# A third joint product in seven weight pairs, with six loads' weight sums kept in DRAM

## Chip, cores, metric

One core of a Trainium2 chip. The metric is the device time of one execution in microseconds (us), lower is better. Kernels are compared only within the same rounds.

## The reference

A linear-attention block gated by a SwiGLU feed-forward block, on 2048 tokens of 1024 features:

```python
xn = _layernorm(x)
s  = _A_ref(xn, A_wqkv, A_wo)          # q, k, v; phi = elu+1; o = q(kv)/q(z); @ wo
g  = silu((silu(xn @ w_gate) * (xn @ w_up)) @ w_down)   # w_gate, w_up: 1024 x 3584
out = x + s * g
```

## The kernel before

The kernel works on two token halves, one after the other. Each weight product is a two-level scheme of the Strassen kind: a "set" has seven products (1 to 7) in place of eight, each of 4 matmuls of 512 columns. Two sets that share their input form a "pair" (gate n, up n, q n, or s n, the attention output). Products 1 and 5 of the two sets are done together, as an inner scheme of the same kind: seven inner products of two matmuls of 256 columns, 14 short matmuls in place of 8 long ones, 3584 columns in place of 4096.

```python
class Joint:                                   # one joint product, four steps a..d
    def step(self, part):
        if part == 0:
            self.grp(1, y, 0, True); self.grp(5, y, 1)
            act(... ps[x][:, 0:256], ps[y][:, 0:256], Identity)   # ACT copies
            act(... self.s, ps[y][:, 256:512], Identity)
        elif part == 1: self.grp(6, y, 0); self.grp(2, x, 0); tt(... ALU.add)
        elif part == 2: self.grp(7, y, 0); self.grp(3, x, 1); tt(... ALU.add); self.put(0, x)
        elif part == 3: self.grp(4, y, 0); self.put(1, y)
# the order in which a pair's head is threaded into the tail of the pair ahead
LINK = "7_0 nj1a 3_0 7_1 nj1b nj5a 3_1 nj1c nj5b 4_0 nj1d nj5c 4_1 n2_0 nj5d n6_0 n2_1 n6_1".split()
```

The price is sums of weights on VectorE. For each 1 MB load, `wload` makes four sums of 128x1024, and for each joint product four inner sums of 128x256:

```python
sums({(k, i): v[...] ...}, [cv[:, q] for q in range(4)], [sr], cr)
for m in joint:                                # joint = (1, 5)
    sums(A, [tv[:, q] for q in range(4)], [r], tr)
```

A planner written in Python orders all instructions at build time, with WINDOW (how many TensorE groups it looks ahead) and LEAD (how early transfers are issued) as constants.

Of the kernel before, what the change touches and what calls it, by code (L numbers as in the profile page):

```python
# [9 lines left out]
ACT = mybir.ActivationFunctionType  # L10
# [4 lines left out]
KB = 1024  # L15
# [19 lines left out]
class Plan:  # L35
# [91 lines left out]
    def tune(self):  # L127

        self.place()
        front = 0.0  # L130
        while True:
            prev, last, work, at = {}, {}, 0.0, None
# [187 lines left out]
def build_kernel(nc, A_x, A_wqkv, A_wo, B_w_gate, B_w_up, B_w_down, out, WINDOW=6, NWARM=15, NPE=2, LEAD=12.0):  # L320
# [12 lines left out]
    with ExitStack() as es:  # L333
# [250 lines left out]
        class Set:  # L584
# [4 lines left out]
            def __init__(self, ops, evac, dring):  # L589
                self.ops, self.evac, self.dring, self.direct = ops, evac, dring, None  # L590

# [16 lines left out]

            def put1(self, a):
                self.a = a  # L610
                self.b = balloc()
                act([bank_r[a]], [bank_r[self.b]], ps[self.b][:, :], ps[a][:, :], ACT.Identity)

            def put5(self, e):
# [93 lines left out]
        TAIL = "7_0 3_0 7_1 4_0 3_1 4_1".split()  # L708
        LINK = "7_0 nj1a 3_0 7_1 nj1b nj5a 3_1 nj1c nj5b 4_0 nj1d nj5c 4_1 n2_0 nj5d n6_0 n2_1 n6_1".split()
        last_pair = [None]  # L710

        def feed(pair):

            prev = last_pair[0]
            if pair is None or not pair.joint:
                if prev is not None:
                    for w in TAIL:
                        prev.do(w)
                if pair is not None:
                    for w in HEAD:  # L720
                        pair.do(w)
            else:
                for w in LINK:
                    if w[0] == "n":
                        pair.do(w[1:])
                    elif prev is not None:
                        prev.do(w)
            last_pair[0] = pair

# [385 lines left out]

        def wload(src, joint, dt=BF16, rd=(), inh=(0, 0)):
            if inh[0]:
# [10 lines left out]
            if inh[1]:  # L1128
                cs, keys = strips("T1", FP16)
                cv = cs.rearrange("p (m w) (kt n) -> p m w kt n", w=2, n=128)  # L1130
                cr = [Region(keys[2 * q] + keys[2 * q + 1]) for q in range(4)]
            else:
                c = cmb_ring.take()
                cv = c.ap(FP16).rearrange("p (m w kt n) -> p m w kt n", m=4, w=2, n=128)
                cr = [c.sub(q * 2 * KB, 2 * KB).r for q in range(4)]
            sums({(k, i): v[:, :, 4 * k:4 * k + 4, i * 128:i * 128 + 128] for k in range(2) for i in range(2)},
                 [cv[:, q] for q in range(4)], [sr], cr)

            def block(m):
# [8 lines left out]
            inner = {}  # L1148
            for m in joint:
                bl, r = block(m)  # L1150
                t = in_ring.take()
                tv = t.ap(FP16).rearrange("p (m kt n) -> p m kt n", m=4, n=128)
                tr = [t.sub(q * KB // 2, KB // 2).r for q in range(4)]
                A = {(k, i): bl[:, i, 2 * k:2 * k + 2, :] for k in range(2) for i in range(2)}
                sums(A, [tv[:, q] for q in range(4)], [r], tr)
                inner[m] = (A, r, tv, tr)
# [18 lines left out]

        def x_inner(v, xin=xin, places=IN_AT):

            for m, at in zip((1, 5), places):
                ap, r = v[XOF[m]]
                B = {(k, j): ap[:, 2 * k:2 * k + 2, 256 * j:256 * j + 256] for k in range(2) for j in range(2)}  # L1180
                t = [(a.at(o, KB, FP16).rearrange("p (k t) -> p k t", t=256), a.reg(o, KB)) for a, o in at]
                tt([r], [t[1][1]], t[1][0], B[1, 1], B[0, 1], ALU.subtract, True)
                tt([r], [r], B[0, 1], B[0, 1], B[0, 0], ALU.subtract, True)
                tt([r], [t[0][1]], t[0][0], B[1, 1], B[0, 1], ALU.subtract, True)
                tt([r, t[0][1]], [t[2][1]], t[2][0], B[1, 0], t[0][0], ALU.subtract, True)
                xin[m] = {1: (B[0, 0], r), 2: (B[1, 0], r), 3: (B[1, 1], r), 5: (B[0, 1], r), 6: t[0], 7: t[1], 4: t[2]}

        def joint_of(jstat, s0, s1, xin=xin):
            def ops(m):
                def f(k):  # L1190
                    ws, wr = jstat(m, k)
                    xa, xr = xin[m][k]
                    return [(ws[q], xa[:, q, :]) for q in range(2)], [wr, xr]
                return f
            return {"1": Joint(ops(1), lambda w, b: (s0, s1)[w].put1(b)),
                    "5": Joint(ops(5), lambda w, b: (s0, s1)[w].put5(b))}
# [17 lines left out]
        def q_load(p, s):  # L1214
            return wload(wqkv_v[:, :, s * 512:(s + 1) * 512], QJ[p][s])

# [4 lines left out]
        def q_pair(p, s, stats, at, go=True):  # L1221
# [8 lines left out]
            s0, s1 = (xset(stat, w, XV[p], evac(w), d_ring) for w in range(2))  # L1230
            pair = Pair(s0, s1, joint_of(jstat, s0, s1) if QJ[p][s] else None, at)
            if go:
# [55 lines left out]

        def gu_load(k, n):
            return wload((wg_v if k == "g" else wu_v)[:, :, n * 512:(n + 1) * 512], (1, 5), inh=(1, 1) if gate[0] and (k, n) == ("g", 0) else (0, 0))  # L1290

        sgs = {}

        def gu_pair(p, kind, n, stats, at):
# [9 lines left out]
            def ev_u(w):  # L1304
                def f(i, j, ap, r, bank):
                    s = sgs[w, i, j]
                    o, orr = hb(2 * n + w, "R%d%d" % (i, j))
                    act([r], [orr], o, ap, ACT.Identity)
                    tt([orr, s.r], [orr], o, o, s.ap(FP16), ALU.mult, True)
                    if w == 1 and (i, j) == (0, 0) and n in TJ_CUT:  # L1310
                        tj_first(p, TJ_CUT[n], n + 1)
                    if w == 1 and (i, j) == (0, 1):
                        h_sums(2 * n)
                return f

            def direct(w):
                def f(i, j, b, s5):
                    s = sgs[w, i, j]
                    o, orr = hb(2 * n + w, "R%d%d" % (i, j))
                    tt([bank_r[b], s5.r], [orr], o, ps[b][:, :], s5.ap(F32), ALU.add)  # L1320
                    tt([orr, s.r], [orr], o, o, s.ap(FP16), ALU.mult, True)
                return f
            s0, s1 = (xset(stat, w, XV[p], (ev_g if kind == "g" else ev_u)(w), d_ring) for w in range(2))
            if kind == "u":
                s0.direct, s1.direct = direct(0), direct(1)
            feed(Pair(s0, s1, joint_of(jstat, s0, s1), at))

# [6 lines left out]

        def s_load(n):
            return wload(m_v[:, :, n * 512:(n + 1) * 512], (1, 5), FP16, [named("mscr", n, g, k) for g in (0, 4) for k in range(4)])

# [15 lines left out]
        GB = 3584  # L1353
        TJ_CUT = {2: 0, 5: 3, 6: 6}
        NU = NPAIR // 2
# [305 lines left out]
        def down(p):  # L1661
# [7 lines left out]
            for seq, prev, nxt in ((IN_D, last_pair[0], d0), (ON_D, d0, d1), (END_D if p else OUT_D, d1, None)):  # L1669
                if seq == END_D:  # L1670
                    PL.cushion = 4.0
                for t in seq.split():
# [16 lines left out]
                    elif t[0] == "n":  # L1689
                        nxt.do(t[1:])  # L1690
                    else:
                        prev.do(t)
            last_pair[0] = nxt

# [8 lines left out]
        def pump(n):  # L1703
            while lq and len(got) < n and lq[0][1] <= gate[0]:
                k, p, s = lq.popleft()
                got[k, p, s] = q_load(p, s) if k == "q" else s_load(s) if k == "s" else gu_load(k, s)

# [10 lines left out]
        def turn_pass():  # L1718
# [9 lines left out]
            gate[0] = 1  # L1728
            raw_ring.__init__([(X, 0), (W, 0 * KB), (X, 0), (W, 8 * KB), (W, 16 * KB)] + [(W, 0), (W, 8 * KB), (W, 16 * KB)] * 5, 8 * KB)
            cmb_ring.__init__([(X, 8 * KB), (X, 8 * KB)] + [(W, 24 * KB), (W, 32 * KB)] * 8, 8 * KB)  # L1730
            in_ring.__init__([(W, 14 * KB), (TM, 8 * KB), (W, 24 * KB), (W, 26 * KB), (W, 42 * KB), (W, 44 * KB)]
# [6 lines left out]
        for p in range(2):  # L1738
            for k, n in order:
# [4 lines left out]
                if p == 0 and (k, n) in (("g", 0), ("u", 0), ("q", 1)):  # L1744
                    at = {"6_1": [build_m]}
                    if k == "u":
                        at["6_0"] = [build_m]
                if (p, k, n) == (0, "g", 1):
                    for q in range(4):
                        dma([P.reg(q * 4 * KB, 4 * KB)], [named("xscr", q)], x_scr[q], P.at(q * 4 * KB, 4 * KB, FP16),  # L1750
                            dsem("xp%d" % q), 512 * KB, after=PL.lastpe)
                if (k, n) == ("u", 1):
                    at = {"j1d": [partial(recip, p)]}
                if (k, n) == ("g", 2):
                    at = {"j1a": [partial(normalise_part, p, 0, 0)], "2_1": [partial(normalise_part, p, 0, 1)]}
                if (k, n) == ("u", 2):
                    at = {"j1a": [partial(normalise_part, p, 1, 0)], "2_1": [partial(normalise_part, p, 1, 1)], "4_1": [partial(combos, QV)]}
                if (k, n) == ("g", 3):
                    at = {"2_1": [partial(x_inner, QV, qin, QIN_AT)]}
                if last_pair[0] is not None and (p, k, n) == (1, "q", 0):  # L1760
                    pass
                elif k == "q":
                    q_pair(p, n, st, at)
                elif k == "s":
# [75 lines left out]
```

## Time and profile before

| | before |
|---|---|
| median, first runs | 712.4 us (711.8 to 713.31) |
| span of the profiled execution | 710.2 us |
| PE (TensorE) busy | 704.5 us, 4181 matmuls |
| VectorE (DVE) busy | 631.2 us, 1534 instructions |
| ScalarE (ACT) busy | 424.9 us |
| moved by DMA | 98.64 MB |

### The profile page before, as it was taken

Reading aid. Unit: us, or ns where it says so; the run is one execution under the profiler, and the core shown is the slowest. Engines: PE = TensorE matmul, PEld = TensorE weight load, DVE = VectorE, ACT = ScalarE, POOL = GpSimd, SP = SyncE. Lnnn points to the kernel's source line nnn. Section 1 sums busy time; section 2 is a strip of 40 time slices with the busy share of each in tenths; the row PEclk is TensorE's granted clock in tenths of the full one; section 3 lists DMA queues with packets and bytes.
Section 4 is the critical chain, followed back from the end, with each engine's and each line's share of the span. In section 5 each row is a group of like instructions: output and inputs, shape, how many; then the busy total and the mean of one; then the engine's idle time right before and its main releaser. Section 6 shows DMA issues by size and latency. Waiting matters only on the chain.

```text
span 710.2 us, 11444 instructions
## 1 busy us (share of the span) xinstructions
PE 704.5 (99%) x4181; PEld 388.1 (55%) x4181; DVE 631.2 (89%) x1534; ACT 424.9 (60%) x827; POOL 13.0 (2%) x34
## 2 busy tenths in 40 slices
PE   8999999999999999999999999999999999999997
PEld 3444445555555555556556455555555555565654
DVE  6999858989999999998958999999999999798863
ACT  5788766988679676664212257876886756531212
POOL 2111000000000000000000000000000000000000
PEclk9999999999999999999999999999999999999999
DMA  9654133346664253326498854322716241646763
GB/s 301 143 95 115 31 118 120 119 133 194 175 181 147 96 160 108 110 63 174 123 243 212 219 133 148 111 68 94 208 60 193 75 149 60 181 138 160 144 156 96
DMA packets 140871, 98.64 MB, mean 139 GB/s; under 512 B 34960, under 2 KB 137872, under 8 KB 140816
## 3 DMA queue, kind: packets, MB, share of 16 engines
q1 hardware_dynamic: 139472, 96.69, 49.1%
q10 hardware_dynamic: 1344, 1.25, 0.5%
q8 instruction: 32, 0.52, 0.3%
q14 instruction: 23, 0.19, 0.1%
HBM read 77.59 MB, written 12.71 MB: 127 GB/s over the span
## 4 chain that ended last, share of the span: by engine, by line
PE 98%; DMA 1%; SPq 0%; issue 0%; DVE 0%; ACT 0%
PE ps L309 98%; DMA H<-in_A_wqkv_dram 1%; PE ps L316 0%; DVE TM L453 0%; SPq L456 0%; SPq L760 0%; ACT TM L442 0%
## 5 line engine op out<-in xcount | busy, mean ns | idle before, releaser
L309 PE MATMUL ps<-X,W 128*128 128x512 f16 (+2 forms) x1348 | 282.6, 349 | 0.0
L442 ACT ACTIVATE TM<-ps 128x512 f16<-128x512 f32 (+3 forms) x386 | 202.7, 554 | 100.8 <-PE ps L309 97.3
L309 PE MATMUL ps<-H,W 128*128 128x512 f16 (+2 forms) x1096 | 218.6, 351 | 0.1
L309 PEld LDWEIGHTS ps<-X,W 128*128 128x128 f16 (+1 forms) x1348 | 130.0, 98 | 101.6 <-ACT H L442 1.0
L453 DVE TENSOR_TENSOR W<-W 128x256 f16<-128x256 f16 (+5 forms) x400 | 178.8, 479 | 2.7 <-PE ps L309 1.9
L309 PEld LDWEIGHTS ps<-H,W 128*128 128x128 f16 (+1 forms) x1096 | 105.9, 98 | 95.4 <-DVE ps L453 1.1
L453 DVE TENSOR_TENSOR ps<-ps,TM 128x256 f32<-128x256 f32 (+1 forms) x250 | 131.4, 527 | 14.8 <-PE ps L309 11.5
L442 ACT ACTIVATE ps<-ps 128x512 f32<-128x512 f32 (+1 forms) x174 | 85.7, 493 | 89.9 <-PE ps L309 89.4
L442 ACT ACTIVATE H<-ps 128x512 f16<-128x512 f32 (+1 forms) x132 | 78.5, 605 | 37.8 <-PE ps L309 37.8
L309 PE MATMUL ps<-P,W 128*128 128x256 f16 (+1 forms) x492 | 94.5, 318 | 0.0
L453 DVE TENSOR_TENSOR H<-H 128x1024 f16<-128x1024 f16 (+5 forms) x130 | 73.7, 581 | 0.7 <-ACT H L442 0.5
L442 ACT ACTIVATE TM<-TM 128x512 f16<-128x512 f32 (+1 forms) x70 | 44.0, 631 | 45.6 <-DVE TM L453 45.1
L309 PEld LDWEIGHTS ps<-P,W 128*128 128x128 f16 (+1 forms) x492 | 47.9, 98 | 27.0 <-ACT TM L442 0.8
L309 PE MATMUL ps<-W 128*128 128x256 f16 (+1 forms) x326 | 61.2, 282 | 0.0
L453 DVE TENSOR_TENSOR H<-H,TM 128x512 f16<-128x512 f16 (+1 forms) x120 | 48.0, 417 | 8.5 <-ACT H L442 8.3
L453 DVE TENSOR_TENSOR TM<-ps,TM 128x512 f32<-128x512 f32 (+3 forms) x63 | 41.6, 660 | 12.9 <-PE ps L309 12.0
L309 PEld LDWEIGHTS ps<-W 128*128 128x128 f16 (+1 forms) x326 | 31.1, 98 | 31.0 <-DVE ps L453 0.8
L309 PE MATMUL ps<-H,X 128*128 128x512 bf16 (+1 forms) x150 | 35.2, 379 | 0.4 <-DMA H<-in_A_wqkv_dram 0.4
L453 DVE TENSOR_TENSOR TM<-TM 128x512 bf16<-128x512 f16 (+2 forms) x73 | 29.2, 412 | 6.1 <-ACT TM L442 4.4
L309 PE MATMUL ps<-H,P 128*128 128x512 bf16 (+1 forms) x110 | 26.8, 379 | 0.0
L453 DVE TENSOR_TENSOR H<-ps,TM 128x512 f16<-128x512 f32 (+1 forms) x35 | 24.0, 686 | 2.2 <-PE ps L309 1.3
L453 DVE TENSOR_TENSOR TM<-TM,W 128x512 f16<-128x512 f16 (+1 forms) x39 | 14.1, 363 | 11.8 <-ACT TM L442 11.7
(111 smaller groups left out, 417.0 us busy)
## 6 DMA issues: line engine op xcount, KB each, us to landing
W<-in_B_w_up_dram SPq DMA_DIRECT2D x14, 1024.0 KB, 5.6
W<-in_B_w_gate_dram SPq DMA_DIRECT2D x13, 1024.0 KB, 5.3
W<-in_B_w_down_dram SPq DMA_DIRECT2D x14, 896.0 KB, 6.1
H<-r_scratch SPq DMA_DIRECT2D x32, 128.0 KB, 3.9
W<-m_scratch SPq DMA_DIRECT2D x4, 1024.0 KB, 5.4
s_scratch<-TM SPq DMA_DIRECT2D x32, 128.0 KB, 2.0
TM<-in_A_x_dram SPq DMA_DIRECT2D x16, 256.0 KB, 4.0
W<-in_A_x_dram SPq DMA_DIRECT2D x15, 256.0 KB, 3.4
```

The lines of the kernel that those rows point to most:

```text
L309: last = h.matmul(o, l, r, start=st, stop=sp, skip_group_check=True)
L442: q = PL.op("act", reads, writes, lambda h: h.activation(o, i, func, **kw), nel(o) / (1000.0 if "bias" in kw or not isinstance(kw.get("sca ...
L453: return dve(reads, writes, lambda h: h.tensor_tensor(o, a, b, op), nel(o), 1.92 if fast else 0.96)
```

## The change

In the second token half, seven pairs do product 2 jointly too. To make room on VectorE for the extra inner sums and additions, six loads store their weight sums to DRAM in the first half and load them in the second. The core of the diff:

```diff
+LINK3 = "7_0 nj1a 3_0 7_1 nj1b nj5a 3_1 nj1c nj5b 4_0 nj1d nj5c 4_1 nj2a nj5d n6_0 nj2b n6_1 nj2c".split()
+w_scr = nc.dram_tensor("w_scratch", [18, 128, 4 * KB], FP16)
+i_scr = nc.dram_tensor("i_scratch", [18, 2, 128, KB], FP16)
+TWO = [('g', 1), ('u', 1), ('g', 3), ('g', 4), ('u', 4), ('g', 5), ('u', 5)]
+NOSP = [('q', 0), ('g', 0), ('u', 0), ('q', 1), ('g', 2), ('u', 2), ('s', 1), ('u', 6), ('g', 6), ('u', 5), ('g', 5), ('u', 4)]
+CH, IH, put = {}, {}, {}
 ...
+            keep = (kind, n) not in NOSP
+            if p and keep:
+                dma([named("ws", kept)], [cl], call, ...)          # second half: load the sums
+            else:
+              sums(...)
+              if keep:                                              # first half: store them,
+                put.setdefault((kind, n), []).append((CH.get((kind, n), "j1a"), lambda: dma(   # at step j1a
+                    [cl], [named("ws", kept)], w_scr[kept], call, ...)))
-            for m in joint:
+            for m in joint + ((2,) if p and (kind, n) in TWO else ()):
 ...  (the inner blocks of products 1 and 5 likewise; one spare copy of product 1 goes to SBUF
 ...   in place of PSUM and is added to product 2 by VectorE; buffers of the second half move;
 ...   the planner's improvement loop is capped at 90 rounds)
```

NOSP lists the loads that are not kept; what remains is gate 1, 3, 4, up 1, 3 and s 0.

More of the change, by code (lines that the diff above doesn't have):

```diff
@@ L130, in tune @@
         front = 0.0
-        while True:
+        for _ in range(90):
             prev, last, work, at = {}, {}, 0.0, None
@@ L589, in __init__ @@
             def __init__(self, ops, evac, dring):
-                self.ops, self.evac, self.dring, self.direct = ops, evac, dring, None
+                self.ops, self.evac, self.dring, self.direct, self.two = ops, evac, dring, None, False
             def out(self, i, j, b):
@@ L609, in put1 @@
             def put1(self, a):
+                if self.two:
+                    self.b = a
+                    self.s1 = s1_ring.take()
+                    act([bank_r[a]], [self.s1.r], self.s1.ap(F32), ps[a][:, :], ACT.Identity)
+                    return
                 self.a = a
@@ L612, in put1, with put2 @@
                 act([bank_r[a]], [bank_r[self.b]], ps[self.b][:, :], ps[a][:, :], ACT.Identity)
+            def put2(self, x):
+                if self.direct is not None:
+                    self.direct(0, 0, x, self.s1)
+                    bfree(x)
+                    return
+                d = d2_ring.take()
+                tt([bank_r[x], self.s1.r], [d.r], d.ap(F32), ps[x][:, :], self.s1.ap(F32), ALU.add)
+                bfree(x)
+                self.evac(0, 0, d.ap(F32), d.r, None)
             def put5(self, e):
@@ L722, in feed @@
             else:
-                for w in LINK:
+                for w in LINK3 if "2" in pair.joint else LINK:
                     if w[0] == "n":
@@ L727, in feed @@
                         prev.do(w)
+                    if w == "7_0" and prev is not None and prev.joint and "2" in prev.joint:
+                        prev.do("j2d")
             last_pair[0] = pair
@@ L1114, in strips, with wload @@
                     [hb(n, nm)[1].keys for n in range(8)])
-        def wload(src, joint, dt=BF16, rd=(), inh=(0, 0)):
+        w_scr = nc.dram_tensor("w_scratch", [18, 128, 4 * KB], FP16)
+        i_scr = nc.dram_tensor("i_scratch", [18, 2, 128, KB], FP16)
+        s1_ring, in2_ring, d2_ring = (Places([(a, o * KB) for a, o in at], 2 * KB) for at in (
+            [(H, 36), (H, 38), (H, 36), (H, 38), (H, 36), (H, 38), (H, 72), (H, 74), (H, 72), (H, 74), (H, 72), (H, 74), (H, 72), (H, 74)],
+            [(H, 42), (H, 44), (H, 42), (H, 68), (H, 70), (H, 76), (H, 78)],
+            [(H, 46), (X, 14), (H, 46), (X, 14), (H, 80), (H, 82), (H, 80), (H, 82)]))
+        TWO = [('g', 1), ('u', 1), ('g', 3), ('g', 4), ('u', 4), ('g', 5), ('u', 5)]
+        NOSP = [('q', 0), ('g', 0), ('u', 0), ('q', 1), ('g', 2), ('u', 2), ('s', 1), ('u', 6), ('g', 6), ('u', 5), ('g', 5), ('u', 4)]
+        CH, IH, put = {}, {}, {}
+        def wload(src, joint, tag, dt=BF16, rd=(), inh=(0, 0)):
+            p, kind, n = tag
+            kept = {"g": 0, "u": 7, "s": 14, "q": 16}[kind] + n
             if inh[0]:
@@ L1128, in wload @@
             if inh[1]:
-                cs, keys = strips("T1", FP16)
+                cs, keys = strips((None, "T1", "T3")[inh[1]], FP16)
                 cv = cs.rearrange("p (m w) (kt n) -> p m w kt n", w=2, n=128)
                 cr = [Region(keys[2 * q] + keys[2 * q + 1]) for q in range(4)]
+                call, csem = cs, dsem("wch%d" % inh[1])
             else:
@@ L1135, in wload @@
                 cr = [c.sub(q * 2 * KB, 2 * KB).r for q in range(4)]
-            sums({(k, i): v[:, :, 4 * k:4 * k + 4, i * 128:i * 128 + 128] for k in range(2) for i in range(2)},
+                call, csem = c.ap(FP16), dsem("wc%s%d" % (c.a.name, c.off // KB))
+            cl = Region(sum((r.keys for r in cr), ()))
+            keep = (kind, n) not in NOSP
+            if p and keep:
+                kv = w_scr[kept]
+                dma([named("ws", kept)], [cl], call, kv.rearrange("p (b t) -> p b t", t=512) if inh[1] else kv, csem, 1024 * KB)
+            else:
+              sums({(k, i): v[:, :, 4 * k:4 * k + 4, i * 128:i * 128 + 128] for k in range(2) for i in range(2)},
                  [cv[:, q] for q in range(4)], [sr], cr)
+              if keep:
+                put.setdefault((kind, n), []).append((CH.get((kind, n), "j1a"), lambda: dma(
+                    [cl], [named("ws", kept)], w_scr[kept], call, dsem("wk%s%d" % (c.a.name, c.off // KB)), 1024 * KB,
+                    after=PL.lastpe)))
             def block(m):
@@ L1148, in wload @@
             inner = {}
-            for m in joint:
+            for m in joint + ((2,) if p and (kind, n) in TWO else ()):
                 bl, r = block(m)
-                t = in_ring.take()
+                t = (in2_ring if m == 2 else in_ring).take()
                 tv = t.ap(FP16).rearrange("p (m kt n) -> p m kt n", m=4, n=128)
@@ L1154, in wload @@
                 A = {(k, i): bl[:, i, 2 * k:2 * k + 2, :] for k in range(2) for i in range(2)}
-                sums(A, [tv[:, q] for q in range(4)], [r], tr)
+                place = "%s%d" % (t.a.name, t.off // KB)
+                held = named("wi", kept, m)
+                if p and m != 2 and keep:
+                    dma([held], [t.r], t.ap(FP16), i_scr[kept, m // 5], dsem("wi" + place), 256 * KB)
+                else:
+                    sums(A, [tv[:, q] for q in range(4)], [r], tr)
+                    if not p and keep:
+                        put.setdefault((kind, n), []).append((IH.get((kind, n), "j%da") % m, partial(
+                            dma, [t.r], [held], i_scr[kept, m // 5], t.ap(FP16), dsem("wj" + place), 256 * KB)))
                 inner[m] = (A, r, tv, tr)
@@ L1174, in build_kernel, with x_inner @@
         xin, qin = {}, {}
-        def x_inner(v, xin=xin, places=IN_AT):
-            for m, at in zip((1, 5), places):
+        def x_inner(v, xin=xin, places=IN_AT, ms=(1, 5)):
+            for m, at in zip(ms, places):
                 ap, r = v[XOF[m]]
@@ L1182, in x_inner, with joint_of @@
                 tt([r], [t[1][1]], t[1][0], B[1, 1], B[0, 1], ALU.subtract, True)
-                tt([r], [r], B[0, 1], B[0, 1], B[0, 0], ALU.subtract, True)
-                tt([r], [t[0][1]], t[0][0], B[1, 1], B[0, 1], ALU.subtract, True)
+                f, fr = t[3] if len(t) > 3 else (B[0, 1], r)
+                tt([r], [fr], f, B[0, 1], B[0, 0], ALU.subtract, True)
+                tt([r, fr], [t[0][1]], t[0][0], B[1, 1], f, ALU.subtract, True)
                 tt([r, t[0][1]], [t[2][1]], t[2][0], B[1, 0], t[0][0], ALU.subtract, True)
-                xin[m] = {1: (B[0, 0], r), 2: (B[1, 0], r), 3: (B[1, 1], r), 5: (B[0, 1], r), 6: t[0], 7: t[1], 4: t[2]}
-        def joint_of(jstat, s0, s1, xin=xin):
+                xin[m] = {1: (B[0, 0], r), 2: (B[1, 0], r), 3: (B[1, 1], r), 5: (f, fr), 6: t[0], 7: t[1], 4: t[2]}
+        def joint_of(jstat, s0, s1, xin=xin, two=False):
             def ops(m):
@@ L1194, in ops @@
                 return f
-            return {"1": Joint(ops(1), lambda w, b: (s0, s1)[w].put1(b)),
+            s0.two = s1.two = two
+            js = {"2": Joint(ops(2), lambda w, b: (s0, s1)[w].put2(b))} if two else {}
+            return {**js, "1": Joint(ops(1), lambda w, b: (s0, s1)[w].put1(b)),
                     "5": Joint(ops(5), lambda w, b: (s0, s1)[w].put5(b))}
@@ L1214, in q_load @@
         def q_load(p, s):
-            return wload(wqkv_v[:, :, s * 512:(s + 1) * 512], QJ[p][s])
+            return wload(wqkv_v[:, :, s * 512:(s + 1) * 512], QJ[p][s], (p, "q", s))
         def pq_tile(g, j):
@@ L1230, in q_pair @@
             s0, s1 = (xset(stat, w, XV[p], evac(w), d_ring) for w in range(2))
-            pair = Pair(s0, s1, joint_of(jstat, s0, s1) if QJ[p][s] else None, at)
+            pair = Pair(s0, s1, joint_of(jstat, s0, s1, two=p == 1 and ("q", s) in TWO) if QJ[p][s] else None, at)
             if go:
@@ L1287, in hb2, with gu_load @@
             return v, Region(hb(n, nm)[1].keys + hb(n + 1, nm)[1].keys)
-        def gu_load(k, n):
-            return wload((wg_v if k == "g" else wu_v)[:, :, n * 512:(n + 1) * 512], (1, 5), inh=(1, 1) if gate[0] and (k, n) == ("g", 0) else (0, 0))
+        def gu_load(p, k, n):
+            return wload((wg_v if k == "g" else wu_v)[:, :, n * 512:(n + 1) * 512], (1, 5), (p, k, n), inh={("g", 0): (1, 1), ("u", 0): (0, 2)}.get((k, n), (0, 0)) if p else (0, 0))
         sgs = {}
@@ L1309, in f @@
                     tt([orr, s.r], [orr], o, o, s.ap(FP16), ALU.mult, True)
-                    if w == 1 and (i, j) == (0, 0) and n in TJ_CUT:
-                        tj_first(p, TJ_CUT[n], n + 1)
+                    if w == 1 and (i, j) == (0, 0) and n in TJ_CUT[p]:
+                        tj_first(p, TJ_CUT[p][n], n + 1)
                     if w == 1 and (i, j) == (0, 1):
@@ L1321, in f @@
                     tt([orr, s.r], [orr], o, o, s.ap(FP16), ALU.mult, True)
+                    if w == 1 and (i, j) == (0, 0) and n in TJ_CUT[p]:
+                        tj_first(p, TJ_CUT[p][n], n + 1)
                 return f
@@ L1325, in gu_pair @@
                 s0.direct, s1.direct = direct(0), direct(1)
-            feed(Pair(s0, s1, joint_of(jstat, s0, s1), at))
+            feed(Pair(s0, s1, joint_of(jstat, s0, s1, two=p == 1 and (kind, n) in TWO), at))
         def h_sums(n):
@@ L1332, in h_sums, with s_load @@
             tt([v["R11"][1], v["T1"][1]], [v["T2"][1]], v["T2"][0], v["R11"][0], v["T1"][0], ALU.subtract, True)
-        def s_load(n):
-            return wload(m_v[:, :, n * 512:(n + 1) * 512], (1, 5), FP16, [named("mscr", n, g, k) for g in (0, 4) for k in range(4)])
+        def s_load(p, n):
+            return wload(m_v[:, :, n * 512:(n + 1) * 512], (1, 5), (p, "s", n), FP16, [named("mscr", n, g, k) for g in (0, 4) for k in range(4)])
         st_ring = Places([(TM, o * KB) for o in (20, 24, 21, 25)], KB)
@@ L1353, in build_kernel @@
         GB = 3584
-        TJ_CUT = {2: 0, 5: 3, 6: 6}
+        TJ_CUT = ({2: 0, 5: 3, 6: 6},) * 2
         NU = NPAIR // 2
@@ L1692, in down @@
                         prev.do(t)
+                        if t == "7_0" and isinstance(prev, Pair) and "2" in prev.joint:
+                            prev.do("j2d")
             last_pair[0] = nxt
@@ L1705, in pump @@
                 k, p, s = lq.popleft()
-                got[k, p, s] = q_load(p, s) if k == "q" else s_load(s) if k == "s" else gu_load(k, s)
+                got[k, p, s] = q_load(p, s) if k == "q" else s_load(p, s) if k == "s" else gu_load(p, k, s)
         pump(2)
@@ L1728, in turn_pass @@
             gate[0] = 1
-            raw_ring.__init__([(X, 0), (W, 0 * KB), (X, 0), (W, 8 * KB), (W, 16 * KB)] + [(W, 0), (W, 8 * KB), (W, 16 * KB)] * 5, 8 * KB)
-            cmb_ring.__init__([(X, 8 * KB), (X, 8 * KB)] + [(W, 24 * KB), (W, 32 * KB)] * 8, 8 * KB)
+            raw_ring.__init__([(X, 0), (W, 0 * KB), (X, 8 * KB), (W, 8 * KB), (W, 16 * KB)] + [(W, 0), (W, 8 * KB), (W, 16 * KB)] * 5, 8 * KB)
+            cmb_ring.__init__([(X, 8 * KB)] + [(W, 24 * KB), (W, 32 * KB)] * 8, 8 * KB)
             in_ring.__init__([(W, 14 * KB), (TM, 8 * KB), (W, 24 * KB), (W, 26 * KB), (W, 42 * KB), (W, 44 * KB)]
@@ L1744, in build_kernel @@
                 if p == 0 and (k, n) in (("g", 0), ("u", 0), ("q", 1)):
-                    at = {"6_1": [build_m]}
+                    at["6_1"] = [build_m]
                     if k == "u":
                         at["6_0"] = [build_m]
+                for w, fn in put.pop((k, n), ()):
+                    at.setdefault(w, []).append(fn)
                 if (p, k, n) == (0, "g", 1):
@@ L1752, in build_kernel @@
                 if (k, n) == ("u", 1):
-                    at = {"j1d": [partial(recip, p)]}
+                    at.update({"j1d": [partial(recip, p)]})
                 if (k, n) == ("g", 2):
-                    at = {"j1a": [partial(normalise_part, p, 0, 0)], "2_1": [partial(normalise_part, p, 0, 1)]}
+                    for w, fn in (("j1a", partial(normalise_part, p, 0, 0)), ("2_1", partial(normalise_part, p, 0, 1))):
+                        at.setdefault(w, []).insert(0, fn)
                 if (k, n) == ("u", 2):
-                    at = {"j1a": [partial(normalise_part, p, 1, 0)], "2_1": [partial(normalise_part, p, 1, 1)], "4_1": [partial(combos, QV)]}
+                    for w, fn in (("j1a", partial(normalise_part, p, 1, 0)), ("2_1", partial(normalise_part, p, 1, 1)), ("4_1", partial(combos, QV))):
+                        at.setdefault(w, []).insert(0, fn)
                 if (k, n) == ("g", 3):
-                    at = {"2_1": [partial(x_inner, QV, qin, QIN_AT)]}
+                    at.setdefault("2_1", []).append(partial(x_inner, QV, qin, QIN_AT))
+                if p == 1 and (k, n) in TWO and "2_1" in at:
+                    at["6_1"] = at.pop("2_1")
                 if last_pair[0] is not None and (p, k, n) == (1, "q", 0):
@@ L1762, in build_kernel @@
                 elif k == "q":
+                    if (p, n) == (1, 1) and TWO:
+                        x_inner(XV[1], places=(((X, 1536), (X, 2560), (X, 5 * KB), (X, 6 * KB)),), ms=(2,))
                     q_pair(p, n, st, at)
```

## The prediction

> **What bounds the kernel now.** I read the page from the top: busy times, slices, then the chain that ended last, and after that the list of who waited for whom on PE.
>
> ```profile
> PE 704.5 (99%) x4181; PEld 388.1 (55%) x4181; DVE 631.2 (89%) x1534; ACT 424.9 (60%) x827; POOL 13.0 (2%) x34
> PE   8999999999999999999999999999999999999997
> PE 98%; DMA 1%; SPq 0%; issue 0%; DVE 0%; ACT 0%
> ```
>
> ```profile
> PE ps L309 <- DVE TM L574: 1.0, 1, 1.0
> PE ps L316 <- DVE W L798: 0.7, 1, 0.7
> PE ps L316 <- DVE TM L453: 0.6, 1, 0.6
> PE ps L309 <- DMA H<-in_A_wqkv_dram: 0.4, 1, 0.4
> ```
>
> The four lines are all the waits that PE has in the whole execution: 2.7 us, from the warm-up and the first tiles. After that PE never waits; 98% of the chain is matmuls. DVE at 89% is near full but hides behind PE. A busy PE need not be at its best pace, so I look at the pace: the PE timeline, columns start, length, instructions.
>
> ```profile
> 445.20 0.38 PE L309 MATMUL ps<-P,X 128*128 128x256 f16 x2
> 445.42 0.38 PE L309 MATMUL ps<-P,W 128*128 128x256 f16 x2
> 445.63 0.38 PE L309 MATMUL ps<-P,TM 128*128 128x256 f16 x2
> 445.85 1.03 PE L309 MATMUL ps<-P,X 128*128 128x512 f16 x4
> 446.72 0.38 PE L309 MATMUL ps<-W 128*128 128x256 f16 x2
> ```
>
> Lengths overlap, so the starts count. Six 256-column matmuls start between 445.20 and 445.85: 0.65/6 = 0.108 us each. Four of 512 columns take 446.72 - 445.85 = 0.87 us: 0.217 each. The pace is proportional to the columns; no semaphore wait shows between the groups. The loads in the DMA queue's timeline give the length of one gate/up pair, because each is issued when the pair three places earlier leaves its buffer:
>
> ```profile
> 579.90 0.38 SPq L456 DMA_DIRECT2D W<-in_B_w_gate_dram  x1
> 591.61 0.38 SPq L456 DMA_DIRECT2D W<-in_B_w_up_dram  x1
> ```
>
> 11.71 us. From the code, one pair is two Strassen sets of seven products; products 1 and 5 of the two sets are done jointly, as an inner seven-product scheme of 14 matmuls of 256 columns each, and the other five are 2 x 4 matmuls of 512 columns. That is 40 x 0.2165 + 28 x 0.1085 = 8.66 + 3.04 = 11.70 us: the pair is nothing but its matmuls' columns.
>
> **What the Trainium skill says.** "TensorE: Matmul & The Clock Gate", section "Back-to-back issue gap", gives N/2.4 + 2.5 ns for a warm matmul by itself: 215.8 ns at 512 and 109.2 at 256. The trace agrees within 1% (217, 108). The same section says a sustained stream reaches about 131 ns at 512; this trace does not (217). "Perfetto Trace Analysis", section "Identifying the Most-Contended Engine", warns that matmul busy share does not measure the distance to the roofline; hence the column count above. "VectorE: DVE Perf Modes", section "The perf-mode tier table", has tensor_tensor at twice the base rate for 16-bit SBUF operands and at the base rate if any is in PSUM: here 128x512 takes 417 ns all in SBUF and 686 to 696 with a PSUM operand. "DMA: Bandwidth & Descriptors", section "Bandwidth", has 6.15 us for 1 MB from HBM; here the 1 MB weight loads land 5.3 to 5.6 us after issue.
>
> **The change, part by part.** I counted the instructions of the two built programs.
>
> (a) Joint product two. Seven pairs of the second token half (gate 1, 3, 4, 5 and up 1, 4, 5) replace 8 matmuls of 512 columns by 14 of 256. The counts fit: 512-column matmuls 2469 to 2413 (-56), 256-column ones 1386 to 1484 (+98). In PE time: -56 x 0.2165 + 98 x 0.1085 = -12.12 + 10.63 = -1.49 us with the trace's pitches; with the skill's two numbers -12.08 + 10.70 = -1.38. I take -1.45. All of it lies on the path, since the chain is PE. (The change was announced to me as eight pairs; the counts show seven in this build.)
>
> (b) Kept sums. Six loads (gate 1, 3, 4, up 1, 3, and one half of the second-token attention output) store their four 128x1024 sums and two inner blocks to DRAM in the first half and load them in the second. DVE loses 24 instructions of 128x1024 and 48 of 128x256. Back to back these cost 0.60 and 0.20 us (two of 0.68 us end after 1.28): 24 x 0.60 + 48 x 0.20 = 24.0 us. DMA gains 6 x (1 MB + 2 x 256 KB) each way, 36 issues, 9.4 MB written and 9.4 read.
>
> (c) What the joint product costs beside PE. DVE: 28 inner sums of 128x256 (5.6), 14 additions of 128x256 from PSUM (14 x 0.34 = 4.8), 14 final additions of 128x512 from PSUM (14 x 0.61 = 8.5), four sums of x (1.4): 20.3 us. DVE is thus about 3.7 us lighter in total, 12 instructions fewer. ACT: 14 more copies of 128x256 (381 ns), 6 fewer evacuations of 128x512 (0.60): +1.7 us on an engine that is 60% busy. Both are beside PE and worth nothing by themselves; the purpose of (b) is to make room for (c).
>
> (d) The planner's improvement loop is now capped at 90 rounds; I counted 23 rounds in the build of the kernel before and 22 in the changed one. The cap does nothing.
>
> Sum: -1.45 us on 712.4 gives 710.95 us if no new wait appears.
>
> **The rivals.** The windows of the second half show what stands near its limit (stretch, length, then busy PE, PEld, DVE, ACT, POOL, clock, DMA share, GB/s):
>
> ```profile
> 503.50:515.00 11.50, 11.50 (x69) 6.58 (x68) 11.49 (x31) 9.95 (x20) 0.00 (x0) 1.00 0.86 210
> 549.50:561.00 11.50, 11.50 (x69) 6.49 (x67) 11.50 (x30) 7.58 (x16) 0.00 (x0) 1.00 0.45 143
> 584.00:595.50 11.50, 11.50 (x68) 6.48 (x67) 10.39 (x27) 7.75 (x16) 0.00 (x0) 1.00 0.27 84
> 607.00:618.50 11.50, 11.50 (x69) 6.48 (x68) 7.78 (x15) 7.75 (x16) 0.00 (x0) 1.00 0.54 152
> ```
>
> *DVE becomes the bound locally.* Up 4, gate 5 and up 5 have joint product two but still form all their sums: each adds about 4 x 0.20 + 2 x 0.34 + 2 x 0.61 = 2.7 us to an 11.5 us pair, 8.1 us for the three. Gate 4 adds 2.7 and saves 4 x 0.60 + 8 x 0.20 = 4.0. From 545 to 618 us that is +6.8 us net against some 6.6 us that DVE had idle there: full to the brim. For it: DVE at 11.50 of 11.50. Against it: windows of 100% DVE already run today with no PE wait, and weight sums can be made ahead of time. If PE followed DVE I would expect 0.5 to 2 us back: 711.5 to 713.
>
> *DMA is late.* The three loads in a row gate 3, up 3 and the attention half fall at 498 to 533 us, where the reciprocals' broadcasts already make 0.86. At about 300 GB/s each kept load (1.57 MB) adds some 5.2 us of DMA time; the three windows from 492 had 19 us of 34.5 in use (0.50, 0.86, and 0.29 after), so about 35 of 34.5. A sum that lands late stops PE outright: 0 to 3 us, so up to 714. Against it: transfers are issued a pair ahead, nothing before it waits on DMA now, and large contiguous rows should move well.
>
> *A shorter lead between joint steps.* Product two now needs four steps with an ACT copy and two DVE additions between them, and two PSUM banks more for a time; they are interleaved with 512-column products of 0.87 us, about the length of two copies of 0.38 plus signalling. Small gaps of 0.1 us in seven pairs would eat up to half the gain: 711.7.
>
> *More than the columns comes back.* It cannot: PE has no waits to remove after the first 10 us. Below 710 would be noise between runs.
>
> **Range and chances.** The planner that orders both programs has so far left no gap on PE after the start, so I expect most of the 1.45 us, less about 0.15 for gaps: 711.1 us. The runs before spread over 711.8 to 713.3, so 0.5 us on a median is noise; the high side gets the rivals. Range 710.1 to 712.8. Two per cent is 14.2 us, ten times the whole effect in either direction; only a stall in every pair could reach it, hence 1% for faster and 2% for slower.
>
> **What will show it.** Right: PE busy time down by 1.3 to 1.5 us with 42 more matmuls; PE's list of waits still only the four of the start, within 0.3 us; up and gate pairs with joint product two 0.2 us shorter; DVE near 628 us, 1522 instructions; about 19 MB more moved by DMA. Wrong: PE waits on sums from DRAM or on DVE between 490 and 620 us, a lower granted clock, or a different pitch of 256-column matmuls when there are more of them.

## More of the kernel before

The chain that ended last, in order of time (start, length, what), shows the two halves:

```profile
125.45 224.40 PE ps L309 x1400
...
349.88 293.82 PE ps L309 x1732
...
643.73 60.97 PE ps L309 x340
...
707.00 0.24 PE ps L316
```

In the first half PE does not leave the chain from 125.45 us on. From 349.88 to 643.73 us it runs nearly the whole second half's weight products without a break: 293.85 us.

A second mark is the first of the small 32x32 matmuls, which comes before anything that the change touches; timeline of PE:

```profile
135.87 0.44 PE L309 MATMUL ps<-H 32*32 32x512 bf16 x16
```

From there to the start of the last PE instruction at 707.00 us are 571.13 us. I call this the marked stretch. It leaves out the start of the kernel, whose length depends on when the first transfers land.

## The result, and the profile after

Median 712.13 us (711.4 to 714.54, 6 runs), the kernel before 712.34 us (6 runs). The ratio is 1.0002, 95% interval 0.9985 to 1.0019. A ratio is the mean time of one kernel's runs over that of the other's of the same rounds, so not quite the ratio of the medians. The forecast of 711.1 us, range 710.1 to 712.8, holds, but so would it for no gain at all, since the median before lies in the range too; most of the forecast gain cannot be seen. The traces tell where it is.

The page of the changed kernel, busy times and chain:

```profile
PE 702.5 (99%) x4212; PEld 391.3 (55%) x4223; DVE 628.2 (88%) x1522; ACT 424.4 (60%) x835; POOL 12.8 (2%) x34
PE 97%; DMA 1%; ACT 1%; DVE 0%; issue 0%; SPq 0%
```

11 records of matmuls are missing from this trace (4212 of 4223), which makes PE's busy time too small; the weight loads (PEld) are complete. VectorE has the 1522 instructions and 628 us that were forecast. ScalarE is new in the chain, with 1%; about half of it comes from the missing records (before 115 us some steps of PE are 0.43 us, twice the 0.216 of the others, and the chain leaves PE there), the rest is shown below. PE's waits, all of them:

```profile
PE ps L316 <- DVE W L816: 1.2, 1, 1.2
PE ps L309 <- DMA H<-in_A_wqkv_dram: 1.2, 2, 0.7
...
PE ps L309 <- ACT ps L442: 0.2, 1, 0.2
```

(The two left out are those of the warm-up, as before.) The first two lie in the first 12 us and are not the change's: the first weights landed later in this execution. The first small matmul shows how much later, 136.65 against 135.87 us; in the eleven other runs below it comes between 135.17 and 136.51 us, whatever the kernel:

```profile
136.65 0.44 PE L309 MATMUL ps<-H 32*32 32x512 bf16 x16
```

The chain in order of time, from 252 us on:

```profile
252.55 0.60 ACT TM L442
253.15 0.50 ACT ps L442
253.69 10.48 PE ps L309 x58
264.19 1.57 ACT TM L442 x3
265.77 0.50 ACT ps L442
266.31 85.00 PE ps L309 x508
351.34 292.62 PE ps L309 x1774
643.99 60.97 PE ps L309 x340
...
707.26 0.24 PE ps L316
```

Two things are to be read here. The stretch of the second half runs from 351.34 to 643.99 us: 292.65 us where it had 293.85. The change gains **1.20 us** there. And the chain now leaves PE twice late in the *first* half, near 253 and 265 us: PE waits for copies on ScalarE, the second time behind three other copies (264.19 us, 1.57 us long). The list of waits gives these only 0.2 us. The starts in PE's timeline give more:

```profile
265.73 0.38 PE L309 MATMUL ps<-X,W 128*128 128x256 f16 x2
266.31 1.90 PE L309 MATMUL ps<-X,W 128*128 128x512 f16 x8 [0.20 <-ACT ps L442]
```

Two matmuls of 256 columns need 0.22 us from their start to the next group's; here the next group starts 0.58 us after them, a slip of 0.36 us, of which the profile calls 0.20 idle. A matmul is shown for 0.27 or 0.38 us but its successor can start after 0.11 or 0.22, so the shown end covers the first 0.16 us of every stall. I therefore took all stalls below from the starts: the step from one matmul to the next, less the mean step in the second half before, 0.216 us for 512 columns and 0.109 for 256. Such a loss is called a slip here. By that account the two slips are 0.26 and 0.37 us, and all slips of more than 10 ns between 200 and 345 us sum to 1.02 us where they had been 0.36.

The marked stretch is 707.26 - 136.65 = 570.62 us (unrounded starts), 0.51 less than before: 1.20 gained in the second half, 0.69 lost in the first. In this profile the late start hides even that. The engines that I suspected of taking the gain are full but do not hold up PE (for a stretch before, see the prediction; the DMA share adds up the times of packets, so it can pass 1; columns: stretch, length, then busy PE, PEld, DVE, ACT, POOL, clock, DMA share, GB/s):

```profile
503.50:515.00 11.50, 11.50 (x75) 7.10 (x74) 10.97 (x28) 10.20 (x22) 0.00 (x0) 1.00 1.10 290
...
584.00:595.50 11.50, 11.50 (x77) 7.32 (x75) 11.46 (x29) 8.10 (x18) 0.00 (x0) 1.00 0.31 98
```

### The profile page after: what moved, and what is told of

The parts are those of the page before. It is cut to its first block, busy times and chain, and to the rows that moved or that the text cites. A ratio compares the mean times of both kernels' runs of the same rounds, so it can differ in the third digit from the quotient of the medians.

```text
span 710.5 us, 11549 instructions
## 1 busy us (share of the span) xinstructions
PE 702.5 (99%) x4212; PEld 391.3 (55%) x4223; DVE 628.2 (88%) x1522; ACT 424.4 (60%) x835; POOL 12.8 (2%) x34
## 2 busy tenths in 40 slices
DMA packets 146057, 117.55 MB, mean 165 GB/s; under 512 B 35536, under 2 KB 138448, under 8 KB 144464
## 4 chain that ended last, share of the span: by engine, by line
PE 97%; DMA 1%; ACT 1%; DVE 0%; issue 0%; SPq 0%
PE ps L309 96%; DMA H<-in_A_wqkv_dram 1%; ACT TM L442 1%; DVE TM L453 0%; PE ps L316 0%; ACT ps L442 0%; ACT H L442 0%; SPq L456 0%; SPq L778 0%; DVE TM L880 0%; DVE stats L796 0%; DVE W L453 0%; DVE nmean L823 0%; DVE ps L453 0%
## 5 line engine op out<-in xcount | busy, mean ns | idle before, releaser
L309 PE MATMUL ps<-X,W 128*128 128x512 f16 (+2 forms) x1362 | 286.3, 349 | 0.2 <-ACT ps L442 0.2
L442 ACT ACTIVATE TM<-ps 128x512 f16<-128x512 f32 (+2 forms) x385 | 200.7, 551 | 103.8 <-PE ps L309 98.3
L453 DVE TENSOR_TENSOR W<-W 128x256 f16<-128x256 f16 (+5 forms) x336 | 155.2, 491 | 1.4 <-PE ps L309 0.6
L453 DVE TENSOR_TENSOR ps<-ps,TM 128x256 f32<-128x256 f32 (+1 forms) x264 | 136.7, 524 | 19.5 <-PE ps L309 16.5
L442 ACT ACTIVATE ps<-ps 128x256 f32<-128x256 f32 (+2 forms) x167 | 80.3, 482 | 84.8 <-PE ps L309 84.3
L442 ACT ACTIVATE H<-ps 128x512 f16<-128x512 f32 (+2 forms) x140 | 82.6, 605 | 39.1 <-PE ps L309 39.0
L309 PE MATMUL ps<-P,W 128*128 128x256 f16 (+1 forms) x464 | 86.0, 307 | 0.0
L309 PEld LDWEIGHTS ps<-P,W 128*128 128x128 f16 (+1 forms) x464 | 45.0, 98 | 22.2 <-ACT TM L442 1.0
L309 PEld LDWEIGHTS ps<-H,X 128*128 128x128 f16 (+1 forms) x150 | 14.4, 98 | 18.0 <-ACT X L442 1.1
```

The lines of the kernel that those rows point to most:

```text
L309: last = h.matmul(o, l, r, start=st, stop=sp, skip_group_check=True)
L442: q = PL.op("act", reads, writes, lambda h: h.activation(o, i, func, **kw), nel(o) / (1000.0 if "bias" in kw or not isinstance(kw.get("sca ...
L453: return dve(reads, writes, lambda h: h.tensor_tensor(o, a, b, op), nel(o), 1.92 if fast else 0.96)
```

## The experiments

Theory A: the gain arrives in the second half, and the stores, by the order they force on the first half, give half of it back. Theory B: the joint product gains nothing. Theory C: DMA traffic costs the time. All runs were correct, and by the 2% rule the verdict of each is "same". "Marked stretch" is from each run's one trace; the changed kernel has 570.62, the kernel before 571.13. Two traces of one program can differ by more than these effects where transfers land late: 570.98 and 569.42 for late_s0_w7 and its repeat.

| run | this / before, median us | ratio, 95% interval | marked stretch us |
|---|---|---|---|
| again | 712.29 / 712.5 | 1.0000, 0.9985 to 1.0015 | 570.64 |
| no_two | 713.96 / 712.5 | 1.0024, 1.0005 to 1.0043 | 571.93 |
| neither | 711.88 / 712.5 | 0.9995, 0.9979 to 1.0011 | 571.32 |
| lead14 | 712.82 / 712.5 | 1.0001, 0.9983 to 1.0019 | 572.53 |
| late_s0 | 711.58 / 712.12 | 0.9992, 0.9978 to 1.0007 | 572.12 |
| late_s0_w7 | 710.88 / 712.12 | 0.9980, 0.9967 to 0.9993 | 570.98 |
| before_w7 | 711.40 / 712.12 | 0.9989, 0.9977 to 1.0001 | 570.45 |
| no_keep | 718.79 / 712.12 | 1.0096, 1.0083 to 1.0110 | 578.27 |
| light | 711.00 / 712.0 | 0.9984, 0.9970 to 0.9997 | 569.95 |
| light_w7 | 710.03 / 712.0 | 0.9973, 0.9961 to 0.9985 | 569.38 |
| late_again_w7 | 710.22 / 712.0 | 0.9984, 0.9968 to 0.9999 | 569.42 |

**again**: no edit.

> The changed kernel as it is, timed again to narrow the interval. Theory A (the columns' gain of 1.4 us arrives in the second half, and two PE stalls of 0.26 and 0.37 us near 253 and 266 us, which came with the stores, give half of it back): 0.6 to 0.8 us faster than before, ratio near 0.999; the two stalls again at the same places; the first 12 us vary by up to 1 us either way. Theory B (the joint product gains nothing, 14 short matmuls take as long as 8 long ones): ratio 1.000 and a second half as long as before. Theory C (DMA traffic slows the core everywhere): stalls at other places than in the first profile.

Measured: marked stretch 570.64 us, second-half stretch again 1.2 us shorter than before, and slips of 0.26 and 0.37 us at the same two steps (252.3 and 264.8 us). They belong to the program, not to one execution. Theory B falls. The timed ratio of 1.0000 does not contradict a gain of 0.5 us (0.9993), but its interval of 0.3% cannot show it: the expected 0.6 to 0.8 us is not confirmed by the times.

**no_two**: kept sums without the joint product.

```diff
-TWO = [('g', 1), ('u', 1), ('g', 3), ('g', 4), ('u', 4), ('g', 5), ('u', 5)]
+TWO = []
```

> Sums kept in DRAM, no joint product two. Theory A: 1.4 to 1.5 us slower than the changed kernel, 0.6 to 0.8 slower than before (ratio near 1.001); the two stalls near 253 and 266 us still there; 4181 matmuls. Theory B: as fast as the changed kernel. Theory C: the same stalls as the changed kernel in the second half.

Measured: 1.31 us longer than the changed kernel in the marked stretch, 0.80 longer than before, both slips still there (0.26 and 0.37). Its second-half stretch is 293.93 us, as before. So the two slips come with the kept sums, not with the joint product, and the 1.2 us of the second half come with the joint product. The timed interval, too, lies above 1, but its 1.7 us are twice what the trace shows; the profiled run was the fastest of the six (712.44 us, the slowest 717.14), and the rest is open.

**neither**: both parts off.

```diff
-TWO = [...]                      +TWO = []
-NOSP = [..., ('u', 4)]
+NOSP = [..., ('u', 4), ('g', 1), ('u', 1), ('s', 0), ('g', 3), ('u', 3), ('g', 4)]
```

> The changed file with no kept sums and no joint product two; only the few moved buffers of the second half are left. Theory A: the time of before within 0.2 us, no stall near 253 or 266 us. If a part of the change outside the two parts cost something, it would be slower than before here.

Measured: no slip near 253 or 266 us; 571.32 us, with one slip of 0.43 us at 406 us in the hand-over between the halves. Its chain runs back to a transposing transfer of 7.11 us in the hand-over; no other run at this LEAD has it in its chain. Without this slip the stretch would be 0.24 us shorter than before. The moved buffers cost nothing that shows.

**lead14**: the transfers planned earlier, everything else kept.

```diff
-... NPE=2, LEAD=12.0):           +... NPE=2, LEAD=14.0):
```

> The changed kernel with one constant of the planner's (how early transfers are issued) at 14 instead of 12: all stores, loads and joint products stay, the order in the first half changes. Theory A: both stalls near 253 and 266 us gone, 0.6 to 0.7 us faster than the changed kernel and 1.3 to 1.4 us faster than before, ratio near 0.998. Theory C: traffic is the same, so the loss stays.

Measured: both slips gone, as Theory A has it, but the time did not follow: 572.53 us, with new slips of 1.14 us at 407, 0.80 at 511 and 0.65 at 543 us. At 511 us ScalarE waits 0.7 us for a broadcast of the reciprocals from DRAM, and the copies that PE needs queue behind it. That speaks for Theory C in a narrower form, at one place of the second half. The run does not settle more, since LEAD moves all transfers.

**late_s0**: one store some steps later.

```diff
-CH, IH, put = {}, {}, {}
+CH, IH, put = {('s', 0): '7_1'}, {}, {}
```

> The changed kernel with one store moved: the weight sums of the first attention-output load are written to DRAM some steps later in the first half. All traffic, all joint products and the planner's constants stay. Theory A (the first-half loss is an order that the stores force on ScalarE and VectorE): the stalls of 0.26 and 0.37 us near 252 and 265 us are gone; from the first small matmul near 136 us to the last matmul about 569.9 us (before 571.13, changed 570.62); timed ratio near 0.998. Theory C (the bytes stored cost the time): both stalls stay, 570.6 us.

Measured: both slips gone (slips from 200 to 345 us sum to 0.30 us) with the same bytes stored. So it was the place of one store in the order, not the amount of traffic, that cost the first half most of its 0.69 us. How the planner's order turns a store into a late copy on ScalarE was not traced. But the profiled execution has four new slips between 503.8 and 511.5 us, 2.26 us in sum. Its chain names the cause:

```profile
501.76 9.73 DMA H<-r_scratch
511.52 0.72 ACT H L442
512.24 0.27 ACT ps L442
```

and so does its list of waits from 500 to 520 us:

```profile
ACT H L442 <- DMA H<-r_scratch: 3.2, 2, 2.2
...
PE ps L309 <- ACT TM L442: 1.5, 3, 1.0
```

The broadcast takes 9.73 us in this chain, where these transfers had a median of 3.9 us before. PE's copies (512.24 and 512.51 us) come after the broadcast's scaling (511.52 us) in it. The six timed runs fall into two groups: 710.16, 710.40 and 710.99 us; 712.18, 712.91 and 713.05 us. The expected ratio of 0.998 was missed (0.9992).

**late_s0_w7** and its control **before_w7**: one more TensorE group to look ahead, with and without the change.

```diff
-... WINDOW=6, ...                +... WINDOW=7, ...
```

> The same, with the planner allowed to look seven instead of six TensorE groups ahead. Theory A: as the run with the store moved, and the two stalls of 0.19 us near 350 and 643 us gone as well: about 569.5 us between the same marks, ratio near 0.9975, the fastest of all. Theory C: broadcasts for the reciprocals late near 505 us, as in the run with earlier loads, and 0.5 to 2 us of stalls there.

> The kernel before with the planner's view of seven groups, as the control of the previous run: only the two stalls of 0.19 us can go, so 0.35 us faster than before, 570.8 us between the marks, ratio near 0.9995.

Measured: the control gains 0.68 us in the marked stretch, more than the 0.35 expected, so the wider view is worth something by itself. The kernel with the change has slips of 0.21 us at 506 us and 1.45 us at 516 us, the latter with PE itself waiting for kept sums:

```profile
PE ps L309 <- DMA W<-w_scratch: 1.3, 1, 1.3
```

**no_keep**: the joint product without kept sums (NOSP as in "neither", TWO as in the change).

> Joint product two in the same seven pairs but no sums kept in DRAM, so that VectorE must form all of them. Theory A (kept sums are there only to make room on VectorE): PE stalls on VectorE between 505 and 540 us and near 570 and 640 us, 5 to 8 us in sum, ratio near 1.009; first half free of the two stalls. My prediction's estimate of 0 to 2 us for VectorE becoming the bound would hold only with the kept sums. If kept sums were not needed: as fast as the run with the store moved.

Measured: 718.79 us, ratio 1.0096; the marked stretch is 7.1 us longer than before. PE waits on VectorE; the first line is the largest such wait, the second the window where PE is busy for 8.15 of 11.50 us and VectorE for all of it:

```profile
PE ps L309 <- DVE W L453: 3.1, 5, 1.1
```

```profile
526.50:538.00 11.50, 8.15 (x45) 3.56 (x44) 11.50 (x31) 5.76 (x13) 0.00 (x0) 1.00 0.04 13
```

So the kept sums are needed: the joint product alone costs more on VectorE than it saves on PE. (The first half is free of the two slips, as expected; it has two others of 0.31 us at 190 us, which I have not traced.)

**light**, **light_w7** and **late_again_w7**: one kept load less, next to the broadcasts. Theory D: from 500 to 520 us the DMA engines are full, and what lands late there stops PE in some executions.

```diff
-NOSP = [..., ('u', 4)]           +NOSP = [..., ('u', 4), ('g', 3)]
 (with late_s0's edit; light_w7 with WINDOW=7; late_again_w7 is late_s0_w7 unchanged)
```

> The run with the one store moved, and gate 3's sums formed by VectorE again instead of loaded: 1.5 MB less each way, all of it beside the reciprocals' broadcasts (492 to 515 us), five kept loads instead of six, all seven joint products stay. Theory D (in the runs with the store moved the gain was lost to sums and broadcasts landing late, because the DMA engines were full from 500 to 520 us): no PE wait there, 569.9 us from the first small matmul to the last matmul (before 571.13), ratio near 0.998. Rival (VectorE needed gate 3's relief): stalls on VectorE near 510 to 540 us, 1 us or more.

> The same with the planner's view of seven groups. Theory D: 569.5 us between the marks, ratio near 0.9975, 1.0 us faster than the control (before with seven groups); the fastest of all.

> The run with the store moved and seven groups, once more and with all six kept loads, as the partner of the previous one on the same chip. Theory D: the late landing is a matter of the execution, because the engines are full: a PE stall of 0 to 2.5 us between 500 and 520 us, not necessarily the one of 1.45 us that the first profile had; 0 to 1 us slower than with five kept loads on average. If the stall is fixed by the order instead, the same 1.4 to 1.5 us at 516 us again.

Measured: with five kept loads the lists show no wait of PE after the first tiles. The waits of light_w7 on PE are these three, all in the warm-up and first tiles:

```profile
PE ps L316 <- DVE W L816: 1.2, 1, 1.2
PE ps L309 <- DVE TM L574: 1.0, 1, 1.0
PE ps L316 <- DVE TM L453: 0.6, 1, 0.6
```

light has 569.95 us, as forecast, 1.18 us less than before; light_w7 569.38, 1.07 less than its control. ScalarE's wait for the broadcasts is 0.5 and 0.3 us, after 3.2 and 2.3 us in late_s0 and late_s0_w7; the changed kernel's two profiles have none. The repeat with six kept loads had no PE stall in its profile (569.42 us, broadcast wait 0.9 us): the 1.45 us are of the execution, not of the program. Its timed runs show it: 710.04, 710.05, 710.19 and 710.25 us, then 711.38 and 713.01. The five of light_w7 lie within 709.55 to 710.84. Five or six runs are few for a statement on tails, so that gate 3's load is the remedy for the slow executions is a guess, not shown; the DMA share from 503.5 to 515 us is still 1.09. The traces speak against the kept bytes as the whole cause. The twelve broadcasts issued between 497 and 520 us landed after a median of 3.8 us before, 5.9 and 5.5 in the changed kernel, 9.7 in late_s0 and 7.4 in both six-load runs with WINDOW=7, which load the same bytes there; light and light_w7 have 5.8, and so has no_keep, which loads no sums at all (it issues its broadcasts in another order). What sets these times stays open. The median of light_w7, 710.03 us, is the lowest of all, 0.27% below before; the changed kernel had 1.0002 and 1.0000 in its own rounds. Of the 0.27% the wider view brings about 0.1% (before_w7, in other rounds, with an interval that reaches 1.0001).

## Why the prediction was right, and where its working failed

The number fell in the range partly by luck: the range of 710.1 to 712.8 us holds the time before as well. The mechanism has to be judged by the traces.

- *PE is the bound, and only columns count.* Right. Between the two marks of the second half, before, 1000 matmuls of 512 columns take 216.1 ns each from start to start and 699 of 256 columns 109.4 ns.
- *The sum, -1.45 us.* The mechanism is right, the term was too big. I read 108.5 ns for 256 columns from six starts; with the mean of 699 the sum is -56 x 0.2161 + 98 x 0.1094 = -1.38 us. Measured: -1.20 us. The remaining 0.18 us is in the mean step of the short matmuls, 109.7 ns over 797 in the changed kernel (797 x 0.3 ns = 0.24 us). It is small gaps, as the third rival had it: the slips of more than 10 ns in this stretch sum to 0.75 and 0.73 us in the two profiles of the changed kernel, 0.59 before. The rival allowed 0.7 us.
- *"The planner ... has so far left no gap on PE after the start", allowance 0.15 us.* This is the step that failed. The gaps that came cost 0.69 us, and they were in the first half. All three rivals with a cost were looked for in the second half, where the joint products are; I counted the stores' bytes but not their effect on the order of the instructions around them. "no_two" and "neither" show that the kept sums bring the slips, and "late_s0" that one store's place does.
- *"After that PE never waits", and no more than the columns can come back.* Wrong, though the list of waits could not show it: the trace before has slips of 0.19 us at 349.6 and 643.4 us and two more near 234 us, 0.24 in sum. before_w7, without the change, won 0.68 us.
- *VectorE full to the brim from 545 to 618 us.* Only in single windows (11.46 of 11.50 us from 584 us on), and with no PE wait: over the whole stretch its busy time rose from 67.09 to 69.11 of 73.00 us, by 2.0 us and not by the 6.8 that were worked out. "no_keep" shows that the step over the brim is steep: 7.1 us.
- *DMA about 35 of 34.5 us from 492 us on.* Right in size: shares of 0.80, 1.10 and 1.00 make 33.4 us. Neither profile of the changed kernel has a PE stall there; three of the variants' have, 0.8 to 2.3 us. I gave this rival 0 to 3 us. Whether the changed kernel's own longest runs (714.54, 714.77 us) are such executions stays open, since only profiled runs show it.
- *Counts.* VectorE 1522 instructions and 628 us, DMA 117.55 MB (+18.9), as worked out. ScalarE has the 8 instructions more, but is 0.5 us less busy where 1.7 more was expected. PE is busy for 702.9 us in the complete trace of "again", 1.6 less (forecast 1.3 to 1.5).

The forecast of 711.1 us lay 1.0 us under the median. 0.25 us of this is the sum and 0.54 the first half (0.69 less the allowed 0.15); the rest, 0.2 us, is within the spread of the runs before, 711.3 to 713.3.

## What to carry to other kernels

When the bound engine has no gaps left, a change is worth its columns only if every other engine's order still fits; look for the cost also where the change puts its preparation (here the stores in the other half), not only where it puts its work. Read stalls of a few tenths from the starts of matmuls rather than from the list of waits. Before sending kept data through DRAM, see what else the DMA engines carry in the window where it must land: one load of 1.5 MB less there, one store later and one more group of look-ahead together turned a change that showed no gain into 0.27%; the share of the load in it is not shown.

## What the Trainium skill lacked or had wrong

- "TensorE: Matmul & The Clock Gate", section "Back-to-back issue gap", calls N/2.4 + 2.5 ns (215.8 at 512, 109.2 at 256) the gap of an isolated matmul and gives about 131 ns for a sustained stream at 512. In these traces the stream itself runs at the isolated gap: 216.1 ns over 1000 matmuls, 109.4 over 699, each with its own weight load.
- "Perfetto Trace Analysis", section "Tensor Engine Instruction (MATMUL, LD_WEIGHTS)", says that the end of a matmul is estimated. It lacks the consequence: at 0.38 us shown and 0.216 us from start to start, stalls up to 0.16 us show no idle time, and one of 0.37 us shows 0.20.
- "DMA: Bandwidth & Descriptors" has no figure for how late a transfer of 128 KB lands when large ones fill the engines. Here the broadcasts between 497 and 520 us landed after a median of 3.8 us before, with a DMA share of 0.86, and after 5.9 and 9.7 us in the changed kernel and in late_s0, both with a share of 1.10.
